# Weight conversion by VectorE and ScalarE alone, one and a half half chunks a step, in the order of use

## The chip, the core and the metric

The kernel runs on one core of a Trainium2 chip. TensorE (PE in the rows) multiplies matrices, VectorE (DVE), ScalarE (ACT) and GpSimd (POOL) work elementwise, and SyncE's queue (SP) issues the transfers from and to memory. Each engine takes its instructions in the order in which the program wrote them; waits between engines are semaphores. The metric is the device time of one execution in microseconds, median of several.

## What is computed

A block-causal attention (4 batches, 8 heads, 576 positions, head dimension 64, blocks of 64 positions), then two feed-forward layers on the 2304 x 512 result. Queries and keys come as float32, the weights as float64.

```python
def _attn_ref(q, k, v):
    scores = 1.0 / np.sqrt(D) * np.matmul(q, k.transpose(0, 1, 3, 2))
    scores = np.where(block_i >= block_j, scores, -1e9)   # blocks of 64
    attn = np.exp(scores - np.max(scores, axis=-1, keepdims=True))
    attn = attn / (np.sum(attn, axis=-1, keepdims=True) + 1e-09)
    return np.matmul(attn, v)

def _moe_ref(x, w_in, w_out):       # x 2304 x 512, w_in 512 x 2048, w_out 2048 x 512
    g = np.maximum(x @ w_in, 0.0) ** 2
    return g @ w_out

def _moe2_ref(x, w_in, w_out):
    h = x @ w_in
    return (h * np.cos(h)) @ w_out

def reference(**kwargs):
    x = _attn_ref(q, k, v)          # rearranged to 2304 x 512
    return _moe2_ref(_moe_ref(x, ...), ...)
```

## The kernel before

**Attention.** 16 pairs of heads are worked on one after another. Their steps (scores L358, maximum L370, exponential L375, scaling of P by GpSimd L411, transposes L432 with their two parts L437 and L440, weighted values L497, joins L508 to L517) are put in order by a planner, the class Plan: each step has an engine, a cost in microseconds and a rank, and each engine takes of the steps that can start the one of lowest rank. The first `EARLY = 8` half chunks of weights are converted among these steps (add_half), at a rank behind everything else.

**Feed-forward layers.** A layer's hidden units come in 16 chunks of 128, the tokens in blocks (512, 512, 256, 512 and 512 in the first layer, 512, 512, 512, 384 and 384 in the second). A step is one chunk of one block. TensorE does the hidden product of step s (L604, 12 products: four pieces of the model dimension, each as high x high, high x low and low x high) and then the output product of step s - 3 (L668, 12 products). ScalarE and VectorE do the activation between them: in the first layer relu and square (L626, L627), the high part of the result (L616, a cast on ScalarE, "gs high") and its low part (L619 on VectorE, "gs low"); the second layer has cosine work in five more steps. What step s leaves is taken up in steps s + 1 (ScalarE's) and s + 2 (gs low). At the end of a block the next one's values are cut into two parts (xs, L299 and L302), and the finished block is copied out of PSUM (L681, L687).

**Weights.** A float64 weight becomes two float32 parts. A chunk is converted in two halves, w_in's (h = 0, read by the hidden product) and w_out's (h = 1, read by the output product). For a half of 128 x 512 the steps are: load (SyncE), shift L201, mask L208, join L219, sign L231, power L237 (VectorE, integers; the words of a float64 lie side by side, so that these read or write every second word), rebias L214 and fraction L225 (ScalarE), and then on GpSimd the high part L246 (from bits) and the low part L252 (low word times high word). A call of convert() takes up to three halves one stage further: it finishes an old one, begins a new one, loads a third. The main loop calls it twice in each step of the first layer and once in a step of the second. The halves come chunk by chunk, w_in then w_out, first layer then second. Layer 2's weights take the tiles of layer 1's; a half of layer 2 may be begun once its chunk c is below freed[0], which is set after the last block's output product of the chunk:

```python
if begun[0].key >= (1, freed[0]):
    return
```

The loop at its core, before:

```python
if not (layer == 1 and c == LAG - 1):
    for _ in range(2 if layer == 0 else 1):
        convert()
```

In this document "the first layer" is layer 0 of the code and "the second" is layer 1.

## Time and profile before

| | us |
|---|---|
| median of 3 runs | 1051.83 |
| lowest and highest run | 1051.08, 1052.38 |
| span of the profiled execution | 1049.7 |
| TensorE busy | 997.2 (95%) |
| VectorE busy | 675.3 (64%) |
| ScalarE busy | 563.1 (54%) |
| GpSimd busy | 272.3 (26%) |

The profile is one execution; its span runs from its first to its last instruction. Busy shares are averages over stages that have different limits, so stages are read one by one: the attention lies at 0 to 209 us, the first layer at 209 to 635, the second from there to the end. Matmuls overlap, so a duration of 12 products is longer than the distance to the next group; distances between starts are what is added up.

### The profile page before, as it was taken

Reading aid. Unit: us, or ns where it says so; the run is one execution under the profiler, and the core shown is the slowest. Engines: PE = TensorE matmul, PEld = TensorE weight load, DVE = VectorE, ACT = ScalarE, POOL = GpSimd, SP = SyncE. Lnnn points to the kernel's source line nnn. Section 1 sums busy time; section 2 is a strip of 40 time slices with the busy share of each in tenths; the row PEclk is TensorE's granted clock in tenths of the full one; section 3 lists DMA queues with packets and bytes.
Section 4 is the critical chain, followed back from the end, with each engine's and each line's share of the span. In section 5 each row is a group of like instructions: output and inputs, shape, how many; then the busy total and the mean of one; then the engine's idle time right before and its main releaser. Section 6 shows DMA issues by size and latency. Waiting matters only on the chain.

```text
span 1049.7 us, 13810 instructions
## 1 busy us (share of the span) xinstructions
PE 997.2 (95%) x4895; PEld 825.7 (79%) x4895; DVE 675.3 (64%) x1244; ACT 563.1 (54%) x1166; POOL 272.3 (26%) x366
## 2 busy tenths in 40 slices
PE   9999999988799999999999887999999999999998
PEld 7766777776578889988888666778888888899997
DVE  7999998799971112121139999986555655565654
ACT  7999888865663334443345556544334433444433
POOL 6889988644420000000004443210000000000000
PEclk9999999999999999999999998999999999999999
DMA  6333222234420000000003443100100100000000
GB/s 232 123 125 134 94 94 93 94 119 136 143 84 1 1 1 1 1 1 1 1 1 120 142 140 110 51 1 1 41 1 1 41 1 1 9 32 1 31 1 30
DMA packets 18805, 58.56 MB, mean 56 GB/s; under 512 B 1968, under 2 KB 2096, under 8 KB 18736
## 3 DMA queue, kind: packets, MB, share of 16 engines
q1 hardware_dynamic: 18736, 57.68, 16.4%
q8 instruction: 38, 0.62, 0.3%
q14 instruction: 31, 0.25, 0.1%
HBM read 52.95 MB, written 4.72 MB: 55 GB/s over the span
## 4 chain that ended last, share of the span: by engine, by line
PE 61%; DVE 32%; ACT 3%; issue 1%; POOL 1%; DMA 0%; SPq 0%; DVEq 0%; ACTq 0%; POOLq 0%
PE acc L668 29%; PE h L604 28%; DVE raw L219 8%; DVE raw L237 4%; DVE bits L231 4%; DVE nmax L370 3%; DVE PTl L440 3%; DVE raw L201 2%; DVE bits L208 2%; DVE gs L619 2%; DVE sums L400 1%; PE ps L497 1%; PE ps L358 1%; DVE g L637 1%; PE ps L432 1%
## 5 line engine op out<-in xcount | busy, mean ns | idle before, releaser
L604 PE MATMUL h<-xs,w 128*128 128x512 f32 (+2 forms) x1920 | 423.6, 370 | 6.2 <-ACT xs L299 6.2
L604 PEld LDWEIGHTS h<-xs,w 128*128 128x128 f32 x1920 | 346.9, 189 | 63.2 <-issue 6.6
L668 PE MATMUL acc<-gs,w 128*128 128x512 f32 (+1 forms) x960 | 219.7, 376 | 23.4 <-DVE gs L619 23.4
L668 PEld LDWEIGHTS acc<-gs,w 128*128 128x128 f32 x960 | 169.5, 191 | 60.8 <-DVE gs L619 30.6
L668 PE MATMUL acc<-w,gs 128*128 128x512 f32 x864 | 211.1, 391 | 2.2 <-ACT xall L681 1.3
L619 DVE TENSOR_TENSOR gs<-g,gs 128x512 fp32r<-128x512 f32 (+2 forms) x160 | 101.0, 632 | 153.9 <-ACT gs L616 153.8
L668 PEld LDWEIGHTS acc<-w,gs 128*128 128x128 f32 x864 | 161.1, 188 | 36.9 <-DVE gs L619 2.1
L616 ACT CAST gs<-g 128x512 fp32r<-128x512 f32 (+2 forms) x160 | 92.2, 576 | 154.9 <-DVE g L651 95.6
L246 POOL TENSOR_SCALAR w<-bits 128x512 fp32r<-128x512 f32 x64 | 43.3, 677 | 362.0 <-DVE bits L231 357.1
L637 DVE SCALAR_TENSOR_TENSOR g<-turns,h 128x512 f32<-128x512 int32 (+1 forms) x80 | 50.5, 632 | 121.0 <-ACT turns L634 121.0
L219 DVE SCALAR_TENSOR_TENSOR raw<-raw 128x512 int32<-128x512 int32 x64 | 91.1, 1424 | 0.0
L358 PE MATMUL ps<-kB,qB 128*128 128x64 f32 (+7 forms) x256 | 83.0, 425 | 3.8 <-DVE PTl L440 1.0
L411 POOL TENSOR_SCALAR P<-P,rinv 128x64 f32<-128x64 f32 (+2 forms) x144 | 78.6, 563 | 25.5 <-DVE rinv L403 16.4
L214 ACT ACTIVATE bits<-bits,new_bias 128x512 int32<-128x512 int32 x64 | 46.3, 723 | 71.9 <-DVE bits L208 71.8
L626 ACT ACTIVATE g<-h 128x512 f32<-128x512 f32 (+1 forms) x80 | 43.9, 549 | 74.1 <-PE h L604 74.1
L634 ACT ACTIVATE turns<-h 128x512 int32<-128x512 f32 (+1 forms) x80 | 44.1, 552 | 69.1 <-PE h L604 69.0
L432 PEld LDWEIGHTS ps<-ident,P 128*128 128x128 f32 (+1 forms) x400 | 46.6, 139 | 38.7 <-DVE PTl L440 20.1
L252 POOL TENSOR_TENSOR w<-raw 128x512 fp32r<-128x512 f32 x64 | 69.4, 1085 | 23.9 <-issue 21.9
L648 ACT ACTIVATE g<-g,half_pi 128x512 f32<-128x512 f32 (+1 forms) x80 | 54.6, 682 | 37.2 <-DVE g L642 37.2
L375 ACT ACTIVATE P<-ps,nmax 128x64 f32<-128x64 f32 (+7 forms) x128 | 64.6, 506 | 17.5 <-DVE nmax L370 16.4
L432 PE MATMUL ps<-ident,P 128*128 128x128 f32 (+1 forms) x400 | 61.9, 277 | 7.8 <-DVE PTl L440 5.1
L440 DVE TENSOR_TENSOR PTl<-ps,PTh 128x512 fp32r<-128x512 f32 x96 | 64.1, 675 | 3.8 <-ACT PTh L437 3.6
(51 smaller groups left out, 1044.6 us busy)
## 6 DMA issues: line engine op xcount, KB each, us to landing
raw<-in_w_dram SPq DMA_DIRECT2D x64, 512.0 KB, 3.7
qB<-in_qd_dram SPq DMA_DIRECT2D x15, 576.0 KB, 5.1
v_raw<-in_vp_dram SPq DMA_DIRECT2D x16, 320.0 KB, 3.0
kB<-in_kT_dram SPq DMA_DIRECT2D x16, 288.0 KB, 3.2
out_dram<-o SPq DMA_DIRECT2D x8, 512.0 KB, 4.6
out_dram<-o SPq DMA_DIRECT2D x2, 256.0 KB, 2.9
qB<-in_qd_dram SPq DMA_DIRECT2D x1, 384.0 KB, 4.3
qB<-in_qd_dram SPq DMA_DIRECT2D x1, 192.0 KB, 2.9
```

What stands on the lines that cost most here:

```text
L219: nc.vector.scalar_tensor_tensor(out=self.low_word, in0=self.high_word, scalar=23, in1=self.low_word, op0=ALU.logical_shift_left, op1=ALU. ...
L252: nc.gpsimd.tensor_tensor(out=weights[(*self.key, self.h)][:, 1], in0=self.low_word.bitcast(F32), in1=self.high_word.bitcast(F32), op=ALU. ...
L358: nc.tensor.matmul(bank[:, 0:w] if one else wide[:, x, 0:w], lhsT=qB[r][:, i].rearrange("p e d -> p (e d)"), rhs=kB[r][:, x * w : (x + 1) ...
L375: nc.scalar.activation(out=mine if one else mine.rearrange("p (x w) -> p x w", x=2), in_=held(), func=AF.Exp, bias=nmax[i], scale=1.0, acc ...
L411: nc.gpsimd.tensor_scalar(out=mine, in0=mine, scalar1=inverse[:, i - i0 : i - i0 + 1], scalar2=1.0, op0=ALU.mult, op1=ALU.mult,)
L432: nc.tensor.transpose(bank[0:keys, n * 128 : (n + 1) * 128], P[r][:, o : o + keys], ident)
L440: nc.vector.tensor_tensor(out=PT[1][:, at] if keys == 128 else PT[0][keys:128, at], in0=bank[0:keys, 0:w], in1=PT[0][0:keys, at].bitcast(F32),
L604: nc.tensor.matmul(h, lhsT=w[:, a, kk * 128 : (kk + 1) * 128], rhs=xs[kk].parts[:, x], start=(m == 0), stop=(m == 3 * KD - 1),)
L616: nc.scalar.copy(out=gs[:, 0], in_=g)
L619: nc.vector.tensor_tensor(out=gs[:, 1], in0=g, in1=gs[:, 0].bitcast(F32), op=ALU.subtract)
L637: nc.vector.scalar_tensor_tensor(out=g, in0=turns, scalar=-part, in1=start, op0=ALU.mult, op1=ALU.add)
L668: nc.tensor.matmul(dst, lhsT=lhsT, rhs=rhs, start=(c == 0 and m == 0), stop=(c == KF - 1 and m == 2),)
```

## The change

- The high part of a half is a ScalarE copy and the low part a VectorE multiply; GpSimd has no part in the weights any more, neither in the attention's plan nor in the layers.
- The halves are sorted: w_out of chunk c comes beside w_in of chunk c + 3, ahead of it.
- The main loop calls convert() by a pace that adds up: 1.5 a step in the first and the last block of the first layer, 2 in its others, and in the second layer one every two steps.
- Room in the second layer is told by halves: w_in's tile of chunk c is free after the last block's hidden product, w_out's after its output product. The step in which the second layer made no call goes.
- Inside a call, the low part stands after the new half's mask and rebias.

```diff
     loads = [((layer, c), h) for layer in range(2) for c in range(KF) for h in range(2)]
+    loads.sort(key=lambda x: (x[0][0], x[0][1] + LAG * x[1], -x[1]))
     loads.reverse()
-    freed = [0]  # chunks of the second layer that have room
+    freed = [0, 0]
...
+        def room(self):
+            key = (*self.key, self.h)
+            if key not in weights:
+                pool = w_pools[0] if self.key[1] < NA else w_pools[1]
+                weights[key] = pool.tile(
+                    [128, 2, DM], F32R, tag=f"w{self.h}", name=f"w{self.h}"
+                )
+            return weights[key]
+
         def high(self):
...
-            nc.gpsimd.tensor_scalar(
-                out=w[:, 0], in0=self.bits.bitcast(F32), scalar1=1.0, scalar2=0.0,
-                op0=ALU.mult, op1=ALU.add,
-            )
+            nc.scalar.copy(out=self.room()[:, 0], in_=self.bits.bitcast(F32))
 
         def low(self):
-            nc.gpsimd.tensor_tensor(
-                out=weights[(*self.key, self.h)][:, 1], in0=self.low_word.bitcast(F32),
+            nc.vector.tensor_tensor(
+                out=self.room()[:, 1], in0=self.low_word.bitcast(F32),
                 in1=self.high_word.bitcast(F32), op=ALU.mult,
             )
...
         if begun:
-            if begun[0].key >= (1, freed[0]):
+            (layer, c), h = begun[0].key, begun[0].h
+            if layer == 1 and c >= freed[h]:
                 return
...
         if old:
             old.power()
             old.high()
-            old.low()
         if new:
             new.mask()
             new.rebias()
+        if old:
+            old.low()
+        if new:
             new.join()
             later.append(new.fraction)
...
-                plan.add("G", 0.59, rank, x.high, [bits])
-                plan.add("G", 1.45, rank, x.low, [raw, high])
+                plan.add("A", 0.56, rank, x.high, [bits])
+                plan.add("V", 0.6, rank, x.low, [raw, high])
...
+        PACE = {0: 1.5, last: 1.5}
+        owed = 0.0
...
-            if not (layer == 1 and c == LAG - 1):
-                for _ in range(2 if layer == 0 else 1):
-                    convert()
+            if step < len(steps) and i == last:
+                freed[0] = c + 1
+            owed += PACE.get(i, 0.5 if layer == 1 else 2)
+            while owed >= 1:
+                owed -= 1
+                convert()
...
                 if i == last:
-                    freed[0] = c + 1
+                    freed[1] = c + 1
```

**VectorE, first block of the first layer.** Here raw and bits are the words of a half on its way, gs the activation; before, one step from gs low to gs low holds two halves:

```order
L619 TENSOR_TENSOR gs_2305<-g_2304,gs_2305 128x512
L231 SCALAR_TENSOR_TENSOR bits_2373<-raw_2364,bits_2373 128x512
L201 TENSOR_SCALAR raw_2377<-raw_2377 128x512
L237 TENSOR_SCALAR raw_2364<-bits_2373 128x512
L208 TENSOR_SCALAR bits_2404<-raw_2377 128x512
L219 SCALAR_TENSOR_TENSOR raw_2377<-raw_2377 128x512
L231 SCALAR_TENSOR_TENSOR bits_2404<-raw_2377,bits_2404 128x512
L201 TENSOR_SCALAR raw_2408<-raw_2408 128x512
L237 TENSOR_SCALAR raw_2377<-bits_2404 128x512
L208 TENSOR_SCALAR bits_2417<-raw_2408 128x512
L219 SCALAR_TENSOR_TENSOR raw_2408<-raw_2408 128x512
L619 TENSOR_TENSOR gs_2348<-g_2347,gs_2348 128x512
```

and with the change a step with one call (the step before it has two such groups of six):

```order
L627 TENSOR_TENSOR gs_2335<-g_2334,gs_2335 128x512
L233 SCALAR_TENSOR_TENSOR bits_2390<-raw_2382,bits_2390 128x512
L203 TENSOR_SCALAR raw_2395<-raw_2395 128x512
L239 TENSOR_SCALAR raw_2382<-bits_2390 128x512
L210 TENSOR_SCALAR bits_2433<-raw_2395 128x512
L257 TENSOR_TENSOR w0_2431<-raw_2382 128x512
L221 SCALAR_TENSOR_TENSOR raw_2395<-raw_2395 128x512
L627 TENSOR_TENSOR gs_2366<-g_2365,gs_2366 128x512
```

The low part (L257, the w row) has joined VectorE's queue, one in each half; line numbers are those of either file (L203, L210, L221, L233 and L239 are the old L201, L208, L219, L231 and L237).

**ScalarE, the same block.** A step with two halves before, from relu to relu:

```order
L626 ACTIVATE g_2503<-h2_2263 128x512
L627 ACTIVATE g_2503<-g_2503 128x512
L225 ACTIVATE raw_2520<-raw_2520 128x512
L616 CAST gs_2504<-g_2503 128x512
L214 ACTIVATE bits_2572<-bits_2572,new_bias_59 128x512
L225 ACTIVATE raw_2533<-raw_2533 128x512
L214 ACTIVATE bits_2585<-bits_2585,new_bias_59 128x512
```

and a step with two calls in the changed kernel:

```order
L634 ACTIVATE g_2520<-h3_2264 128x512
L635 ACTIVATE g_2520<-g_2520 128x512
L227 ACTIVATE raw_2494<-raw_2494 128x512
L624 CAST gs_2521<-g_2520 128x512
L254 CAST w0_2573<-bits_2532 128x512
L216 ACTIVATE bits_2575<-bits_2575,new_bias_59 128x512
L227 ACTIVATE raw_2537<-raw_2537 128x512
L254 CAST w1_2586<-bits_2575 128x512
L216 ACTIVATE bits_2588<-bits_2588,new_bias_59 128x512
```

The cast of each half's high part (L254) stands between the fraction of its half and the rebias of the next; w0 and w1 alternate, w0 for a later chunk than w1.

**VectorE in the attention.** The stretch at row 266 of its queue, around the join of a pair's values, before:

```order
L237 TENSOR_SCALAR raw<-bits 128x512
L201 TENSOR_SCALAR raw<-raw 128x512
L511 TENSOR_TENSOR xall<-ps_85,half_117 64x320
L208 TENSOR_SCALAR bits<-raw 128x512
L219 SCALAR_TENSOR_TENSOR raw<-raw 128x512
L370 TENSOR_REDUCE nmax_105<-ps_83 128x1
L201 TENSOR_SCALAR raw<-raw 128x512
L440 TENSOR_TENSOR PTl<-ps_86,PTh 128x512
```

and with the change:

```order
L239 TENSOR_SCALAR raw<-bits 128x512
L203 TENSOR_SCALAR raw<-raw 128x512
L519 TENSOR_TENSOR xall<-ps_86,half_117 64x320
L257 TENSOR_TENSOR w_1341<-raw 128x512
L378 TENSOR_REDUCE nmax_105<-ps_87 128x1
L210 TENSOR_SCALAR bits<-raw 128x512
L221 SCALAR_TENSOR_TENSOR raw<-raw 128x512
L378 TENSOR_REDUCE nmax_106<-ps_85 128x1
```

The multiply for a half (L257) stands among the maxima and joins, and the halves on their way are at another stage than before. In the whole attention the queue holds eight such rows; the last stands after row 380 of some 440, where the last conversion row was 325 of 430.

## Rows read from the trace of the kernel before

Timeline rows are: start (us), duration (us), engine, line, operation, out<-in, partitions x elements and type, count; in brackets the idle time before it and what ended it.

**Rows 1.** The page, section 2: VectorE's busy tenths in 40 slices of 26.24 us.
```profile
DVE  7999998799971112121139999986555655565654
```

**Rows 2.** Windows: length; busy us of PE, PEld, DVE, ACT, POOL; clock; DMA; GB/s.
```profile
26.25:157.50 131.25, 120.41 (x718) 92.98 (x716) 126.46 (x282) 118.07 (x331) 114.57 (x156) 1.00 0.34 114
157.50:209.00 51.50, 48.17 (x305) 38.48 (x303) 43.26 (x103) 44.48 (x125) 40.85 (x59) 1.00 0.28 95
209.04:304.97 95.93, 80.10 (x327) 62.34 (x326) 91.89 (x136) 57.23 (x95) 44.23 (x49) 0.96 0.40 132
635.25:640.23 4.98, 4.98 (x12) 3.71 (x13) 4.98 (x9) 1.96 (x4) 1.41 (x2) 0.56 0.04 16
```

**Rows 3.** Timeline, TensorE, the first layer's first block.
```profile
222.73 2.88 PE L604 MATMUL h<-xs,w 128*128 128x512 f32 x12
...
234.37 2.79 PE L668 MATMUL acc<-gs,w 128*128 128x512 f32 x11 [1.81 <-DVE gs L619]
...
304.97 2.88 PE L604 MATMUL h<-xs,w 128*128 128x512 f32 x12
...
310.41 2.88 PE L604 MATMUL h<-xs,w 128*128 128x512 f32 x12
```

**Rows 4.** Timeline, TensorE, from the first layer's last block into the second layer.
```profile
585.11 2.88 PE L604 MATMUL h<-xs,w 128*128 128x512 f32 x12
...
635.25 5.14 PE L604 MATMUL h<-xs,w 128*128 128x512 f32 x12 [6.22 <-ACT xs L299]
...
689.71 2.88 PE L604 MATMUL h<-xs,w 128*128 128x512 f32 x12
...
696.02 2.88 PE L604 MATMUL h<-xs,w 128*128 128x512 f32 x12
...
701.47 2.88 PE L604 MATMUL h<-xs,w 128*128 128x512 f32 x12
```

**Rows 5.** Timeline, all engines: one half chunk's conversion in the first block.
```profile
264.44 0.68 DVE L231 SCALAR_TENSOR_TENSOR bits<-raw,bits 128x512 int32<-128x512 int32 x1
...
264.85 0.60 ACT L616 CAST gs<-g 128x512 fp32r<-128x512 f32 x1
265.04 0.42 DVE L201 TENSOR_SCALAR raw<-raw 128x512 int32<-128x512 int32 x1
265.21 0.73 POOL L246 TENSOR_SCALAR w<-bits 128x512 fp32r<-128x512 f32 x1 [1.84 <-DVE bits L231]
265.38 0.84 DVE L237 TENSOR_SCALAR raw<-bits 128x512 int32<-128x512 int32 x1
266.14 0.41 DVE L208 TENSOR_SCALAR bits<-raw 128x512 int32<-128x512 int32 x1
266.36 1.09 POOL L252 TENSOR_TENSOR w<-raw 128x512 fp32r<-128x512 f32 x1 [0.42 <-issue]
266.47 1.53 DVE L219 SCALAR_TENSOR_TENSOR raw<-raw 128x512 int32<-128x512 int32 x1
...
267.92 0.68 DVE L231 SCALAR_TENSOR_TENSOR bits<-raw,bits 128x512 int32<-128x512 int32 x1
...
268.52 0.42 DVE L201 TENSOR_SCALAR raw<-raw 128x512 int32<-128x512 int32 x1
```

**Rows 6.** Timeline, the same stretch earlier: L219 with no GpSimd operation beside it.
```profile
212.95 0.68 DVE L219 SCALAR_TENSOR_TENSOR raw<-raw 128x512 int32<-128x512 int32 x1
...
213.96 1.04 POOL L252 TENSOR_TENSOR w<-raw 128x512 fp32r<-128x512 f32 x1 [1.54 <-ACT raw L225]
```

**Rows 7.** Line L231 in the attention: count, duration ns least/median/most, first and last start.
```profile
L231 DVE SCALAR_TENSOR_TENSOR bits<-raw,bits x8: 670/778/1201, 37.7 to 153.6; 128x512 int32<-128x512 int32 x8
```

**Rows 8.** Timeline, VectorE, attention: a pair's widest maximum, one in each pair.
```profile
34.80 0.74 DVE L370 TENSOR_REDUCE nmax<-wide 128x1 f32<-128x576 f32 x1
...
166.00 0.74 DVE L370 TENSOR_REDUCE nmax<-wide 128x1 f32<-128x576 f32 x1
...
189.76 0.75 DVE L370 TENSOR_REDUCE nmax<-wide 128x1 f32<-128x576 f32 x1
```

More of the change, by code (lines that the diff above doesn't have):

```diff
@@ L183, in tile_block_causal_attention__then__two_ffn @@
     weights = {}
+    LAG = 3
     loads = [((layer, c), h) for layer in range(2) for c in range(KF) for h in range(2)]
+    loads.sort(key=lambda x: (x[0][0], x[0][1] + LAG * x[1], -x[1]))
     loads.reverse()
     loaded, begun = [], []
-    freed = [0]
+    freed = [0, 0]
     class Half:
@@ L240, in power @@
             )
-        def high(self):
-            pool = w_pools[0] if self.key[1] < NA else w_pools[1]
-            w = pool.tile([128, 2, DM], F32R, tag=f"w{self.h}", name=f"w{self.h}")
-            weights[(*self.key, self.h)] = w
-            nc.gpsimd.tensor_scalar(
-                out=w[:, 0], in0=self.bits.bitcast(F32), scalar1=1.0, scalar2=0.0,
-                op0=ALU.mult, op1=ALU.add,
-            )
+        def room(self):
[6 more added lines that the diff above has]
+            return weights[key]
+        def high(self):
+            nc.scalar.copy(out=self.room()[:, 0], in_=self.bits.bitcast(F32))
         def low(self):
-            nc.gpsimd.tensor_tensor(
-                out=weights[(*self.key, self.h)][:, 1], in0=self.low_word.bitcast(F32),
+            nc.vector.tensor_tensor(
+                out=self.room()[:, 1], in0=self.low_word.bitcast(F32),
                 in1=self.high_word.bitcast(F32), op=ALU.mult,
@@ L700, in layers @@
         steps = [(i, c) for i in range(len(blocks)) for c in range(KF)]
-        LAG = 3
+        PACE = {0: 1.5, last: 1.5}
+        owed = 0.0
         gss = {}
```

## Prediction

> **What bounds the kernel now.** I began with the page's busy digits in 40 slices [rows 1]. VectorE stands at 9 in three stretches: in the attention (slices 2 to 6), in slices 9 to 11 and in 22 to 26. Then the table of windows [rows 2] put the other engines beside it. Over the first block of the first layer, 209.04 to 304.97, VectorE is busy 91.89 of 95.93 us and TensorE only 80.10; so VectorE sets the pace there, and in the attention's middle it does so at 126.46 of 131.25 us.
>
> The TensorE timeline says what a feed-forward step costs when nothing holds it: from 304.97 to 310.41, 5.44 us (24 products of 512 columns) [rows 3]. In the first block the steps are further apart, and the wait named in front of the output products is gs low, VectorE's last operation on a step's activations: 1.81 us in this row, the same in most steps. From step 4 (222.73) to step 15 (304.97) eleven steps take 82.24 us; at 5.44 they take 59.84. **22.4 us** are lost there. The same happens around the seam of the layers [rows 4]: from step 10 of the first layer's last block (585.11) to step 11 of the second layer's first block (701.47) lie 17 steps in 116.36 us, against 92.48: **23.9 us**. A piece of this is the wait of 6.22 us for the next block's xs at 635.25; TensorE had stood still before it, the granted clock of the next stretch is 0.56 [rows 2], near the level of 1.2 GHz, and twelve products took 5.14 us instead of 2.88. Between these stretches TensorE runs at its pace, and nothing is to be had.
>
> Why VectorE is late stands in a VectorE, GpSimd and ScalarE timeline of one half chunk [rows 5]. VectorE starts L201 at 265.04 and the next half's L201 at 268.52: 3.48 us for a half of five operations. L237 takes 0.84 us where L201 and L208, the same form, take 0.42 and 0.41: GpSimd's L246 runs beside it. L219 takes 1.53 us beside GpSimd's L252. In [rows 6] L219 starts at 212.95 and is over before L252 starts at 213.96: 0.68 us. So GpSimd's two operations per half cost VectorE about 0.85 and 0.42 us, which is more than they would take on VectorE.
>
> **The change part by part.** *Conversion on VectorE and ScalarE.* L246 becomes a cast on ScalarE, priced by the cast of gs, same shape, 0.60 us [rows 5]. L252 becomes a two-input multiply on VectorE, whose nearest row is L231 (two inputs, 128x512), 0.68 us and 0.60 to the next start [rows 5]. Its inputs are every second word; L219 reads and writes like that and takes the same 0.68 [rows 6]. Bounds: 0.41 (L208) and 1.53 (L219 beside GpSimd, [rows 5]); I take 0.60, since no GpSimd is left in the layers. From start to start a half is then 0.60 (L231) + 0.34 (L201) + 0.34 (L237) + 0.34 (L208) + 0.60 (multiply) + 0.60 (L219) = 2.82 us instead of 3.48.
>
> *1.5 half chunks a step.* Before, two: 2 x 3.48 + 0.60 (gs low, also of two inputs) = 7.56 us a step, which is the pace seen. With the change 1.5 x 2.82 + 0.60 = **4.83 us**, under 5.44. A step with two calls takes VectorE 6.24, one with one call 3.42; a gs low is queued a whole step before its product, which covers the 0.8. ScalarE was busy 57.23 us over this stretch with 24 halves; 24 casts of 0.60 make 71.6 of about 79 (four hidden products and one output, then twelve steps of 5.44): high, but under TensorE's time. What stands behind a waiting cast there is the next chunk's relu, whose own product ends later.
>
> *The order of halves.* Slowed to 1.5, the weights must come as the products ask for them. w_in of chunk c is now the (2c-1)th half, w_out of chunk c-3 the one before. Eight are ready at the start, two calls fill the pipe, so after step 12 there are 17, after step 13 19, after step 14 20; steps 13, 14 and 15 ask for 17, 19 and 21, so step 15 forces one more call, ahead of its product. A half cut in step s is done some 3 us into TensorE's step s, 2.4 us before step s+1. So block 0 loses nothing: **-22.4 us**. The loads keep their number on SP's queue, and the fourth raw buffer is free about two calls ahead, as before.
>
> *Room by halves, in the last block.* The first halves of layer 2 wait on hidden products of the same step (chunks 0, 1, 2); behind that wait stand ScalarE's relu, which needs the same product, and a gs low that is due two steps later, so nothing is lost. Three calls return empty; then 1.5 a step, 21 halves at the block's end, and the other 11 in layer 2 at one in two steps. There a step with one half took 6.31 us, from 689.71 to 696.02 [rows 4]; less 3.48 and plus 1.41 it is 4.24, under 5.44. The wait for xs goes too: that cast stands in ScalarE's queue behind the step's conversions, which were late by the pace of 7.56 us a step; at TensorE's pace ScalarE reaches it when step 15's hidden product ends. What is late next is w_out of chunks 14 and 15, which are cut in the very step that uses them, behind VectorE's 4.24 us of work: I put 1.3 us on it, with bounds of nothing and of a whole step, 5. **-23.9 + 1.3**.
>
> *Attention.* Eight halves are cut there, and eight multiplies and eight casts move from GpSimd. With conversion a pair of heads takes (166.00 - 34.80) / 10 = 13.12 us, without it (189.76 - 166.00) / 2 = 11.88 [rows 8]. VectorE is 96% busy in the first case and 84% from 157.50 on [rows 2], so the eight multiplies lie on the path: 8 x 0.60 = 4.8 us. Upper bound: GpSimd still scales P there, and L231, of the same kind, took 0.67 to 1.20 us [rows 7]: 9.6 us. Lower bound: the new order spreads the halves into the pairs after 157.50, where 8.2 us of VectorE lie idle; and 16 GpSimd operations fewer (1.09 and 0.73 us, [rows 5]) relieve what is left, so a gain of 2 us is the other end. The casts, 8 x 0.60 = 4.8 us, go to ScalarE, busy 90% there [rows 2], 8.4 us less than VectorE, so it stays second. I take **+4.5 us**, near the plain 4.8.
>
> *The Trainium skill on this.* The Trainium skill's page SBUF — State Buffer, section "SBUF: two separate sides", says that VectorE and GpSimd share a pair of ports under an exclusive lock, held for the whole instruction, so that whoever comes second waits. By that rule L219 would have ended 0.68 us after L252, at 268.13; the row [rows 5] ends at 268.00, so the trace nearly agrees. The rule speaks against the change in the attention, where GpSimd works on: each multiply could wait out a whole operation, and by 1.09 + 0.68 us for each of eight the attention would pay 14.2 us, the whole sum 1021.
>
> Sum: 1051.83 - 22.4 - 23.9 + 1.3 + 4.5 = **1011.3 us**. The profiled execution has a span of 1049.7, 2.1 under the median of the runs; its stretches are taken off the median as they are.
>
> **The rivals.** *The attention pays double.* Each multiply is held by a GpSimd operation and takes the 1.20 us of [rows 7], and the casts lengthen the same chain: 9.6 + 4.8 us instead of 4.5. For it: VectorE at 96%. Against: L231's median is 0.78, and a pair with conversion is only 1.24 us longer than one without. It gives 1016 to 1021.
>
> *1.5 is too much.* ScalarE at 71.6 of 79 us and VectorE at 4.83 of 5.44 hand each other six results a half; if each of some 27 steps lost half a microsecond, 13.5 us come back: 1025. Against it: before, VectorE ran without a gap at 91.89 of 95.93 us through the same exchange.
>
> *The slow operations are slow by themselves.* If L219 stays at 1.53 and L237 at 0.84 without GpSimd, a half is 3.48 + 0.60 and a step 6.72: block 0 loses 11 x 1.28 = 14.1 and the last block 16 x 1.28 = 20.5 of what is hoped for: 1046. The change then does not do what it says. [rows 6] speaks against it.
>
> *Slower: the room wait closes into a ring.* In the last block the cast and the multiply for chunk c wait for hidden product c on in-order engines. If every step were held like that, its round would be half a step for the hidden product (2.72), five ScalarE operations of about the cast's 0.60 (cast of w, L214, relu, square, cast of gs; 3.0), 0.68 (gs low, as L231) and 2.72 (output), 9.12 us: 3.7 lost in each of 16 steps, 60 us, so 1071. It is slower than before from 2.5 us a step on. Against it: after chunk 2 the room that a half takes was freed one to three steps earlier.
>
> **How the numbers follow.** The forecast 0.62; attention dearer 0.17; 1.5 too much 0.12; slow by themselves 0.05; ring 0.04. The forecast's own spread is 1003.5 (attention -2 and nothing late at the end) to 1020 (attention 9.6, 5 late at the end); I round the lower end to 1004, since both would have to come together. With the first rival whole and most of the second the range is 1004 to 1023. A measurement here tells 0.2%, 2 us. All cases but the last are faster by more: 0.95 faster, 0.01 same, 0.04 slower.
>
> **What the changed kernel's profile would show.** L219's successor at about 0.68 and L237's at 0.41 in the layers; hidden products 5.44 us apart from step 4 on in block 0, and across the seam, with the granted clock at 1.00; no GpSimd after the attention; first hidden product at about 213.5 instead of 209.04. It is wrong if the products still wait for gs low each step, if they wait for w (L246's or L252's successor), or if the attention ends after 219.

## The result and the profile after

| | before | after |
|---|---|---|
| median us | 1052.11 (4 runs beside it) | **1007.55** (4 runs, 1006.25 to 1009.78) |
| ratio, 95% interval | 1 | 0.9578 [0.9564, 0.9592] |
| span of the profiled execution | 1049.7 | 1005.0 |
| TensorE busy, share of the span | 95% | 98% |
| first hidden product at | 209.04 | 207.22 |

The forecast was 1011.3, with a range of 1004 to 1023. The changed file is a little longer, so that lines move: L201 is now L203, L208 L210, L219 L221, L231 L233, L237 L239, L246 L254, L252 L257, L604 L612, L619 L627, L668 L676.

The page of the changed kernel, section 2 (busy tenths in 40 slices of 25.1 us) and section 4 (shares of the chain that ended last):

```profile
DVE  7999999979972121211168979788656645656554
POOL 6878887720000000000000000000000000000000
PEclk9999999999999999999999999999999999999999
...
PE 79%; DVE 14%; ACT 4%; issue 1%; POOL 0%; DMA 0%; SPq 0%; DVEq 0%; ACTq 0%; POOLq 0%
```

VectorE still shows 9 in the attention, as in [rows 1]; at the first block two slices are left of three, at the seam two of five. GpSimd is silent from slice 10 on. The chain runs over TensorE for 79% of the span and over VectorE for 14%, most of the latter in the attention. The windows of the changed kernel give the same stretch by stretch (length, then busy us of PE, PEld, DVE, ACT and POOL, the granted clock, the DMA's share, GB/s):

```profile
26.25:157.50 131.25, 123.53 (x740) 96.00 (x739) 125.51 (x291) 123.68 (x347) 109.64 (x147) 1.00 0.35 117
157.50:207.20 49.70, 45.01 (x286) 36.32 (x285) 45.04 (x103) 42.47 (x118) 38.01 (x51) 1.00 0.27 92
207.22:302.51 95.29, 95.29 (x423) 78.92 (x422) 82.44 (x169) 78.98 (x136) 0.87 (x1) 1.00 0.40 133
```

In the third stretch, which is about as long as the one of [rows 2], TensorE is now busy for all of 95.29 us and VectorE for 82.44; there it was 80.10 and 91.89 of 95.93. It is no longer the first block alone, since that now ends at 286.19; up to there VectorE is busy for 71.66 of 78.97 us. In the attention VectorE has hardly moved, 125.51 of 131.25 us against 126.46.

TensorE's timeline of the changed kernel, at step 4 of the first block and across the seam of the layers, the places of [rows 3] and [rows 4] (start, duration, engine, line; a bracket would be a wait):

```profile
220.91 2.88 PE L612 MATMUL h<-xs,w 128*128 128x512 f32 x12
223.63 2.88 PE L676 MATMUL acc<-gs,w 128*128 128x512 f32 x12
226.35 2.88 PE L612 MATMUL h<-xs,w 128*128 128x512 f32 x12
...
626.17 2.88 PE L612 MATMUL h<-xs,w 128*128 128x512 f32 x12
628.89 2.88 PE L676 MATMUL acc<-w,gs 128*128 128x512 f32 x12
631.61 2.88 PE L612 MATMUL h<-xs,w 128*128 128x512 f32 x12
```

Hidden products start 5.44 us apart, here and in every step from 220.91 to 686.01 whose two products have 512 tokens (once 5.47, at a block's start); the wait for gs and the wait for xs are gone. Then one step stalls. TensorE with what VectorE and ScalarE do ahead of it, in the second layer's first block:

```profile
686.01 2.88 PE L612 MATMUL h<-xs,w 128*128 128x512 f32 x12
...
689.20 0.68 DVE L627 TENSOR_TENSOR gs<-g,gs 128x512 fp32r<-128x512 f32 x1
...
689.80 0.68 DVE L233 SCALAR_TENSOR_TENSOR bits<-raw,bits 128x512 int32<-128x512 int32 x1
...
690.52 0.62 ACT L254 CAST w<-bits 128x512 fp32r<-128x512 f32 x1 [0.42 <-DVE bits L233]
...
691.19 0.50 PE L676 MATMUL acc<-w,gs 128*128 128x512 f32 x1 [2.30 <-ACT w L254]
...
692.15 2.79 PE L676 MATMUL acc<-w,gs 128*128 128x512 f32 x11 [0.45 <-DVE w L257]
...
694.78 2.88 PE L612 MATMUL h<-xs,w 128*128 128x512 f32 x12
```

From hidden product to hidden product this step takes 8.77 us instead of 5.44, so 3.33 are lost. The output product asks for a half that is cut in this very step: its L233 starts at 689.80, behind nine operations of the activation that stand ahead of it in VectorE's queue from 683.86 on (the last is the L627 at 689.20).

**Where the time went.** Three numbers of a trace account for the span of nearly every kernel in this study: when the first hidden product starts, what the first block loses against 5.44 us a step, and what the stretch from the first layer's last block to the end of the second layer's first block loses (the seam of the layers lies in it). What is left of the span is 794.3 to 794.5 us in all but one kernel.

| kernel | median us | ratio, 95% interval | first hidden | lost, block 0 | lost, seam and layer 2 | span |
|---|---|---|---|---|---|---|
| before | 1052.1 | | 209.04 | 22.4 | 23.9 | 1049.7 |
| after | 1007.55 | [0.9564, 0.9592] | 207.22 | 0 | 3.4 | 1005.0 |
| a1_new_order_gpsimd | 1006.97 | [0.9556, 0.9582] | 205.32 | 0 | 5.0 | 1005.2 |
| a2_old_order_new_engines | 1009.98 | [0.9585, 0.9616] | 209.28 | 0 | 3.3 | 1007.0 |
| b1_pace_order_room_gpsimd | 1027.36 | [0.9750, 0.9779] | 209.57 | 12.1 | 8.5 | 1024.6 |
| b2_engines_alone | 1021.48 | [0.9693, 0.9722] | 209.59 | 7.9 | 7.4 | 1019.3 |
| b3_pace2 | 1018.65 | [0.9667, 0.9699] | 207.14 | 7.7 | 6.2 | 1015.5 |
| b4_chunk_order | 1015.37 | [0.9637, 0.9665] | 207.15 | 3.8 | 7.3 | 1012.7 |
| b5_old_room | 1018.15 | [0.9661, 0.9687] | 207.09 | 0 | 15.1 | 1016.5 |
| c1_tail | 1003.19 | [0.9519, 0.9545] | 207.04 | 0 | 0 | 1001.4 |
| c2_gpsimd_beside | 1051.59 | [0.9982, 1.0001] | 206.92 | 25.0 | 23.8 | 1050.0 |
| e1_gpsimd_attention_tail | **1001.68** | [0.9507, 0.9533] | 205.68 | 0 | 0 | 1000.0 |
| e2_early6 | 1001.89 | [0.9511, 0.9537] | 201.89 | 3.9 | 0 | 1000.1 |
| e3_early7 | 1001.89 | [0.9504, 0.9530] | 204.88 | 1.0 | 0 | 1000.3 |

(In a1 the rest is 794.9. The half microsecond more lies behind the last hidden product: from there to the end of the span it is 15.67 us, against 15.14 in the changed kernel. c2's 25.0 has in it 1.1 us of two steps of the second block.) From before to after: 22.4 + 23.9 - 3.4 + 1.8 = 44.7 us, the difference of the spans.

### The profile page after: what moved, and what is told of

The parts are those of the page before. It is cut to its first block, busy times and chain, and to the rows that moved or that the text cites. A ratio compares the mean times of both kernels' runs of the same rounds, so it can differ in the third digit from the quotient of the medians.

```text
span 1005.0 us, 13762 instructions
## 1 busy us (share of the span) xinstructions
PE 982.7 (98%) x4895; PEld 823.0 (82%) x4895; DVE 642.6 (64%) x1308; ACT 595.4 (59%) x1230; POOL 165.1 (16%) x238
## 4 chain that ended last, share of the span: by engine, by line
PE 79%; DVE 14%; ACT 4%; issue 1%; POOL 0%; DMA 0%; SPq 0%; DVEq 0%; ACTq 0%; POOLq 0%
PE h L612 38%; PE acc L676 38%; DVE nmax L378 4%; DVE PTl L448 4%; ACT P L383 1%; PE ps L366 1%; ACT PTh L445 1%; PE ps L505 1%; DVE sums L408 1%; ACT half L516 1%; PE ps L440 1%; DVE g L645 1%; DVE xall L519 1%; DVE raw L203 1%; DVE xs L310 1%
## 5 line engine op out<-in xcount | busy, mean ns | idle before, releaser
L612 PE MATMUL h<-xs,w 128*128 128x512 f32 (+2 forms) x1920 | 420.7, 368 | 0.0
L612 PEld LDWEIGHTS h<-xs,w 128*128 128x128 f32 x1920 | 344.6, 188 | 55.2
L676 PE MATMUL acc<-w,gs 128*128 128x512 f32 x864 | 210.1, 391 | 2.8 <-ACT w L254 2.3
L676 PE MATMUL acc<-gs,w 128*128 128x512 f32 (+1 forms) x960 | 210.2, 368 | 0.0
L676 PEld LDWEIGHTS acc<-gs,w 128*128 128x128 f32 x960 | 168.3, 189 | 30.0
L627 DVE TENSOR_TENSOR gs<-g,gs 128x512 fp32r<-128x512 f32 (+2 forms) x160 | 101.3, 634 | 142.4 <-ACT gs L624 142.2
L676 PEld LDWEIGHTS acc<-w,gs 128*128 128x128 f32 x864 | 161.6, 188 | 35.7 <-ACT w L254 2.7
L419 POOL TENSOR_SCALAR P<-P,rinv 128x64 f32<-128x64 f32 (+2 forms) x144 | 81.7, 584 | 34.1 <-DVE rinv L411 19.8
L505 PE MATMUL ps<-PTh,vhl 128*128 128x320 f32 (+3 forms) x224 | 60.5, 304 | 3.6 <-POOL vhl L480 1.4
L445 ACT CAST PTh<-ps 128x512 fp32r<-128x512 f32 (+1 forms) x112 | 58.8, 543 | 1.1 <-PE ps L440 0.5
L378 DVE TENSOR_REDUCE nmax<-ps 128x1 f32<-128x64 f32 (+7 forms) x128 | 55.4, 445 | 6.0 <-PE ps L366 5.5
```

What stands on the lines that cost most here:

```text
L378: nc.vector.tensor_reduce(out=nmax[i], in_=held(), axis=AX.X if one else AX.XY, op=ALU.max, negate=True)
L419: nc.gpsimd.tensor_scalar(out=mine, in0=mine, scalar1=inverse[:, i - i0 : i - i0 + 1], scalar2=1.0, op0=ALU.mult, op1=ALU.mult,)
L445: nc.scalar.copy(out=PT[0][0:keys, at], in_=plan.held[s][0][0:keys, 0:w])
L505: nc.tensor.matmul(bank[:, (a - i0) * D : w], lhsT=vhl[:, j, e].rearrange("p x d -> p (x d)"), rhs=pt[x][:, s0 : s0 + i1 - a, e, :], start ...
L612: nc.tensor.matmul(h, lhsT=w[:, a, kk * 128 : (kk + 1) * 128], rhs=xs[kk].parts[:, x], start=(m == 0), stop=(m == 3 * KD - 1),)
L627: nc.vector.tensor_tensor(out=gs[:, 1], in0=g, in1=gs[:, 0].bitcast(F32), op=ALU.subtract)
```

## Experiment 1: is it GpSimd's presence that made a half slow?

c2 takes the changed kernel and lets GpSimd do its two former operations again, in the layers, into a tile that nobody reads. VectorE and ScalarE still make the weights.

```diff
+    idle = const.tile([128, DM], F32R, name="idle")
...
             old.high()
+            nc.gpsimd.tensor_scalar(out=idle, in0=old.bits.bitcast(F32), ...)
+            nc.gpsimd.tensor_tensor(out=idle, in0=old.low_word.bitcast(F32), ...)
```

> The changed kernel with GpSimd's two former operations issued again in every call of the layers, on the same inputs, into a tile that nobody reads. Theory (GpSimd running beside VectorE is what made a half dear): the join takes 1.5 us and the power 0.84 again, a half 4.1 us, a step of 1.5 halves 6.7 us; 14 us are lost in the first block and 20 in the last, about 1042. Rival (the operations were dear for where they stood, not for GpSimd): they stay at 0.68 and 0.42, 1008.

Measured: 1051.59 us, all of the gain gone. One half of c2 in the first block, VectorE and GpSimd, and TensorE's wait behind it (here L240 is the power, L222 the join, L258 the multiply, L636 gs low):

```profile
240.23 0.65 POOL L286 TENSOR_SCALAR idle<-bits 128x512 fp32r<-128x512 f32 x1 [1.31 <-DVE bits L234]
240.32 0.84 DVE L240 TENSOR_SCALAR raw<-bits 128x512 int32<-128x512 int32 x1
...
241.40 1.59 POOL L290 TENSOR_TENSOR idle<-raw 128x512 fp32r<-128x512 f32 x1 [0.52 <-DVE raw L240]
241.41 0.68 DVE L258 TENSOR_TENSOR w<-raw 128x512 fp32r<-128x512 f32 x1
...
242.01 1.53 DVE L222 SCALAR_TENSOR_TENSOR raw<-raw 128x512 int32<-128x512 int32 x1
...
244.20 1.20 PE L685 MATMUL acc<-gs,w 128*128 128x512 f32 x4 [2.27 <-DVE gs L636]
```

The join takes 1.53 us again and the power 0.84, the same two numbers as in [rows 5], while the multiply of the same half keeps its 0.68. In the changed kernel one half in the second layer, VectorE alone:

```profile
671.07 0.69 DVE L233 SCALAR_TENSOR_TENSOR bits<-raw,bits 128x512 int32<-128x512 int32 x1
671.67 0.42 DVE L203 TENSOR_SCALAR raw<-raw 128x512 int32<-128x512 int32 x1
672.01 0.42 DVE L239 TENSOR_SCALAR raw<-bits 128x512 int32<-128x512 int32 x1
672.34 0.42 DVE L210 TENSOR_SCALAR bits<-raw 128x512 int32<-128x512 int32 x1
672.68 0.69 DVE L257 TENSOR_TENSOR w<-raw 128x512 fp32r<-128x512 f32 x1
673.28 0.68 DVE L221 SCALAR_TENSOR_TENSOR raw<-raw 128x512 int32<-128x512 int32 x1
```

So the slowness is the neighbour's, not the operation's: the rival "slow by themselves" fell. The price of a half is as expected: from L234 at 239.39 to the next at 244.06 lie 4.67 us with one gs low of 0.60 in them, so a half of c2 costs VectorE 3.48 + 0.60 us, six operations of which two are slowed, and a step of 1.5 halves 6.7. The loss is larger than expected, 25.0 and 23.8 us instead of 14 and 20, and the time 1051.59 instead of 1042. I had multiplied the 1.28 us by which a step exceeds 5.44 by the number of steps; Experiment 2 shows at b1 why that is the wrong sum. Summed as it is done there, 12 steps of 6.72 - 4.83 us make 22.7, and the 22nd join of the block stands at 304.51, 24.1 us behind the changed kernel's 280.37.

## Experiment 2: one part of the change at a time

Four kernels take one part out, or bring one alone. b1 has the new pace, order and room, but GpSimd finishes every half as before:

```diff
-            old.high()
+            old.high_g()
+            old.low_g()
...
-        if old:
-            old.low()
```

> The change's pace of 1.5, its order of halves and its room, with the two last steps of a half on GpSimd as before, in the attention and in the layers (the attention in its old order). Theory (the pace takes off most of the loss by itself, the engines take off the rest): a half is 3.48 us of VectorE as before, a step 1.5 x 3.48 + 0.60 = 5.82 us, 0.38 over TensorE's 5.44, so block 0 gives back some 4 us, the last block some 6, the attention ends at 209 again (+1.8): about 1020. Rival (the engines are what counts, as the run with idle GpSimd work suggests, which lost all 44 us): 1035 to 1050. Rival (pace, order and room do everything): 1009.

b2 is the kernel before with the new engines in the layers alone:

```diff
-            nc.gpsimd.tensor_scalar(out=w[:, 0], in0=self.bits.bitcast(F32), ...)
+            nc.scalar.copy(out=self.room()[:, 0], in_=self.bits.bitcast(F32))
...
-            nc.gpsimd.tensor_tensor(out=weights[(*self.key, self.h)][:, 1], ...)
+            nc.vector.tensor_tensor(out=self.room()[:, 1], ...)
```

> The kernel before with one part of the change: in the layers the high part of a half is ScalarE's cast and the low part VectorE's multiply. Pace 2, order by chunks, room by chunks and the attention stay as before. Theory: a half is 2.82 us, a step 2 x 2.82 + 0.60 = 6.24 us, 0.80 over TensorE's 5.44. Block 0 loses 11 x 0.80 = 9 of the 22.4 us, the last block with the seam 16 x 0.8 = 13 of the 23.9: about 1052 - 46.3 + 22 = 1028. Rival (the slow operations of the half weren't GpSimd's doing): 1052 or more, since VectorE then has one operation more in a half. Rival (engines alone suffice, the pace is nothing): 1007 to 1012.

b3 is the changed kernel at the old pace:

```diff
-        PACE = {0: 1.5, last: 1.5}
+        PACE = {}
```

> The changed kernel with two calls a step in the whole first layer instead of 1.5 in its first and last block. Theory: a step with two halves is 2 x 2.82 + 0.60 = 6.24 us of VectorE, 0.80 over 5.44. In block 0, 24 halves are cut in 12 steps instead of 16, then 0.8 x 12 = 9.6 us are lost; in the last block room limits it, some 13 steps of 0.8, 10: about 1007.5 + 15 to 20 = 1022 to 1027, with the half chunks of the second layer earlier and its stall of 3.3 us gone. Rival (the order and the engines suffice): 1004 to 1008.

b4 leaves the halves in the old order, b5 frees w_in's room as late as w_out's:

```diff
-    loads.sort(key=lambda x: (x[0][0], x[0][1] + LAG * x[1], -x[1]))
```

> The changed kernel with the halves in the old order, chunk by chunk, w_in then w_out, at the pace of 1.5. Theory: w_in of chunk c is then the (2c + 1)th half instead of the (2c - 1)th from chunk 3 on, wanted in step c; of the eight ready at the start and 1.5 a step the wanted half is behind from about step 10 on, and calls are forced just ahead of a product, each half the length of a late half (4 to 5 us): three to four of them in block 0, some in layer 2's first block: 1015 to 1025. Rival (the order doesn't matter): 1007 to 1009.

```diff
-            if step < len(steps) and i == last:
-                freed[0] = c + 1
...
-                    freed[1] = c + 1
+                    freed[0] = freed[1] = c + 1
```

> The changed kernel with room in the second layer told as before: w_in's tile counts as free only after the last block's output product of its chunk, three steps later than the hidden product. Theory (the room by halves is needed): three steps of 1.5 calls return empty, so some four to five halves fewer are ready at the seam, and the second layer, which is given one half in two steps, falls behind the products earlier, at its step 10 or so; from there each step takes two halves, some 3 us more than 5.44 each, four to six of them: 1018 to 1024. Rival (the room by halves is not needed, the forced calls hide): 1006 to 1009.

Measured: engines alone 1021.48, everything but the engines 1027.36, both together 1007.55. Either takes off more than half of the 44 us; they overlap, since both lower VectorE's work in a step. Neither is enough alone. Nor is any part without effect: at two halves a step the kernel stands at 1018.65, in the old order at 1015.37, with the old room at 1018.15.

What each leaves behind is to be seen on TensorE. In b2 and b3 VectorE sets the step again, at 6.24 us (2 x 2.82 + 0.60, as expected), and at the seam the next block's xs is late once more. TensorE of b2, first block and seam:

```profile
244.58 2.79 PE L685 MATMUL acc<-gs,w 128*128 128x512 f32 x11 [0.49 <-DVE gs L636]
...
250.81 2.83 PE L685 MATMUL acc<-gs,w 128*128 128x512 f32 x11 [0.50 <-DVE gs L636]
...
608.21 5.79 PE L621 MATMUL h<-xs,w 128*128 128x512 f32 x12 [4.21 <-ACT xs L316]
```

The two output products lie 6.23 us apart. The last block itself lost nothing in b2 or b3 (its steps stand 5.44 apart up to the seam): VectorE runs late there without TensorE's waiting, and the bill comes with xs, 4.21 us in the row, with twelve products in 5.79 us behind it. That fits what the prediction said of xs at the seam, that it is late by VectorE's and ScalarE's backlog. Since I had counted 0.80 us for each step of the last block, both kernels came out cheaper than expected (1028 for b2, 1022 to 1027 for b3).

In b4 the steps of the first block are 6.22 apart from step 11 on (the row below is of step 12): each of them forces a second half ahead of its product, and TensorE waits for w, not for gs. In b5 the loss of 15.1 us is all behind the seam, where four steps take 7.65 to 11.40 us. Three of them have a wait for w of 2.42 to 2.69 us, like the changed kernel's stall; in the fourth (7.65) it is mostly the clock, ten products in 4.13 us at a granted 0.61 that take 2.56 elsewhere. TensorE of b4:

```profile
266.14 2.56 PE L611 MATMUL h<-xs,w 128*128 128x512 f32 x10 [0.22 <-DVE w L256]
```

b1 is where a step of my reckoning failed. I expected 0.38 us lost in each step of the first block (1.5 x 3.48 + 0.60 = 5.82), some 4 in all. VectorE did keep that pace: its joins at 221.27 and 291.05 are twelve steps apart, 5.82 each. But the block lost 12.1 us. GpSimd and TensorE of b1:

```profile
270.61 0.72 POOL L254 TENSOR_SCALAR w<-bits 128x512 fp32r<-128x512 f32 x1 [1.84 <-DVE bits L233]
...
271.39 0.73 PE L623 MATMUL h<-xs,w 128*128 128x512 f32 x2 [1.35 <-POOL w L254]
...
271.75 1.09 POOL L260 TENSOR_TENSOR w<-raw 128x512 fp32r<-128x512 f32 x1 [0.42 <-issue]
...
272.89 3.86 PE L623 MATMUL h<-xs,w 128*128 128x512 f32 x10 [0.77 <-POOL w L260]
```

TensorE waits for w, the half just cut. (The ten products of the last row take 3.86 us, 2.57 in other steps; the granted clock there is 0.63.) The products ask for two halves a step and VectorE makes one and a half; the eight in stock pay for the rest, and they are used up at the block's end. And VectorE has no idle time to take a loss from: in the changed kernel, too, it runs without a gap from 212.81 to 270.79, with one of 1.14 us behind that. So a loss on any of the halves comes out at the end nearly in full: the changed kernel's VectorE needs 4.83 us a step, b1's 5.82, and 12 steps of 0.99 are 11.9 us. The 22nd join of the block is at 294.53 in b1 and at 280.37 in the changed kernel, 14.2 us apart; the next block's first hidden product is at 300.68 and 286.19, 14.5 apart, and 2.4 of it are the later start of the layers. What decides is the sum of VectorE's work up to the last half that is wanted, not its surplus over 5.44 in a single step.

## Experiment 3: the attention, by its order or by its engines?

The attention was to cost 4.5 us more and ended 1.8 us earlier. The planner was given new engines and costs for the eight halves, and so it also wrote another order. a1 keeps the new order but lets GpSimd finish the halves; a2 keeps the old order (the planner is told the old engines and costs) but lets ScalarE and VectorE finish them. Both have the changed kernel's layers.

```diff
 a1
-                plan.add("A", 0.56, rank, x.high, [bits])
-                plan.add("V", 0.6, rank, x.low, [raw, high])
+                plan.add("A", 0.56, rank, x.high_g, [bits])
+                plan.add("V", 0.6, rank, x.low_g, [raw, high])
 a2
-                plan.add("A", 0.56, rank, x.high, [bits])
-                plan.add("V", 0.6, rank, x.low, [raw, high])
+                plan.add("G", 0.59, rank, x.high, [bits])
+                plan.add("G", 1.45, rank, x.low, [raw, high])
```

> The changed kernel with the attention's eight halves finished on GpSimd again, in the changed kernel's order of steps on every other engine. Theory (work taken off GpSimd frees VectorE, so the engines are what shortened the attention): the first hidden product starts later than 207.2 us, at 209 to 211, and the whole is 1009 to 1011. Rival (the planner's other order is what helped): it starts at 207 or before, the whole is 1007.5 or less. The layers are as in the changed kernel in both.

> The changed kernel with the attention's steps planned as before (order of the kernel before), the eight halves finished on ScalarE and VectorE. Theory (engines): the first hidden product starts at about 207, the whole is 1007 to 1008. Rival (order): it starts at 209 or later, the whole is 1009.5 or more.

Measured, the first hidden products, in this order a2, the changed kernel, a1 (three traces):

```profile
209.28 11.13 PE L612 MATMUL h<-xs,w 128*128 128x512 f32 x48
```

```profile
207.22 11.13 PE L612 MATMUL h<-xs,w 128*128 128x512 f32 x48
```

```profile
205.32 11.13 PE L624 MATMUL h<-xs,w 128*128 128x512 f32 x48
```

With before's 209.04 that is a table of two by two, and other runs repeat three of its cells. The old order with GpSimd gave 209.57 and 209.59 too (b1, b2), the new order with the new engines 206.92 to 207.22 (six kernels), the new order with GpSimd 205.68 too (e1). So the same attention varies by up to 0.55 us, and by that measure:

- the new order gains 2.1 to 2.4 us with ScalarE and VectorE, and 3.4 to 4.3 with GpSimd;
- the new engines cost 1.2 to 1.9 us in the new order, and nothing that can be told from the spread in the old one.

So the earlier end is the order's. The engines gained nothing; they cost at most 1.9 us, less than the 4.5 that I put on them.

*Where the order's gain is.* The last of the eight halves (its power, the last operation that all four kernels have) starts at 154.9 us before and at 154.7 in a2, but at 175.9 in the changed kernel and at 174.5 in a1. The planner, which now counts 0.6 us of VectorE for each, spreads them over some 21 us more, into the stretch in which [rows 2] left 8.2 us of VectorE idle. TensorE is further on by then: up to 157.50 it has been busy for 123.53 us in the changed kernel, 120.41 in [rows 2] and 121.20 in a2. No run moves the halves and leaves the rest of the order alone, so that this place of the gain is argued and not shown.

*Why eight multiplies cost so little.* In a2 VectorE is as busy from 26.25 to 157.50 as before, 126.25 us against 126.46, though seven multiplies are new there. The groups of VectorE's operations in that stretch (count, busy us, mean ns, idle before), first two of a2, then one of before:

```profile
L257 DVE TENSOR_TENSOR w<-raw 128x512 fp32r<-128x512 f32 x7 | 5.3, 757 | 0.0
...
L408 DVE TENSOR_SCALAR sums<-sums 128x4 f32<-128x4 f32 x10 | 4.3, 427 | 0.1
```

```profile
L400 DVE TENSOR_SCALAR sums<-sums 128x4 f32<-128x4 f32 x10 | 7.2, 720 | 0.1
...
L403 DVE RECIPROCAL rinv<-sums 128x4 f32<-128x4 f32 x10 | 1.8, 178 | 1.0
```

The multiplies cost 5.3 us. An operation on four columns took 720 ns on average and takes 427; over ten pairs that gives back 2.9 us, its sisters on two and three columns 1.3, the conversion's own operations the rest. The reciprocal of the same four columns takes 178 ns, so that most of the 720 should be a wait and no work. The trace of before shows the wait, here at its longest:

```profile
80.37 1.54 POOL L472 TENSOR_TENSOR vhl<-v_raw,vhl 128x640 fp32r<-128x640 f32 x1
...
80.48 1.45 DVE L400 TENSOR_SCALAR sums<-sums 128x4 f32<-128x4 f32 x1
```

GpSimd's operation ends at 81.91 and VectorE's at 81.93. Of the 29 operations on sums that start in this stretch, nine take 0.15 to 0.17 us; of the 20 longer ones 18 end 0.02 to 0.04 us behind a GpSimd operation that ran beside them. In 14 of these 18 that was an operation of the attention itself, as in this row, and not the weights' work. So it matters when GpSimd's operations fall more than how many there are: in a1, where GpSimd is busy for 115.91 us of the stretch (114.57 before), the operation on four columns takes 280 ns. What the sums gave back in a2 is therefore at least in part a shift in time, which the prediction had not reckoned.

The Trainium skill, page SBUF — State Buffer, section "SBUF: two separate sides", has a lock between VectorE and GpSimd: whoever starts first keeps the shared pair for a whole instruction. The prediction priced this as a rival that makes each multiply wait, 14.2 us. The multiplies' mean of 757 ns against 0.68 us alone shows that they hardly waited. The sums' ends agree with the rule; the waits that vanished from them were not in that price.

## Experiment 4: the stall in the second layer

c1 cuts a little more in the second layer's first block, so that the last half is ready before its step:

```diff
-        PACE = {0: 1.5, last: 1.5}
+        PACE = {0: 1.5, last: 1.5, last + 1: 0.75}
```

> The changed kernel with 0.75 instead of 0.5 calls a step in the second layer's first block, so that the last two w_out halves are cut a step or more before their products. Theory (the wait of 2.3 us for w in step 17 and the 0.45 and 0.6 us beside it is a half cut too late): step 17 takes 5.44 us instead of 8.77, the whole is 3.3 us shorter, 1004.3. Rival (VectorE is full there anyhow, 2.83 + 0.75 x 2.82 = 4.95 of 5.44 us, and other steps lose it): 1006 to 1008.

Measured: 1003.19 us (1002.87 to 1003.38). TensorE of c1, the place of the stall:

```profile
685.84 2.88 PE L612 MATMUL h<-xs,w 128*128 128x512 f32 x12
688.56 2.88 PE L676 MATMUL acc<-w,gs 128*128 128x512 f32 x12
691.28 2.88 PE L612 MATMUL h<-xs,w 128*128 128x512 f32 x12
694.00 2.88 PE L676 MATMUL acc<-w,gs 128*128 128x512 f32 x12
696.72 2.88 PE L612 MATMUL h<-xs,w 128*128 128x512 f32 x12
```

The step is 5.44 us again. The medians differ by 4.4 us, more than the 3.4 of the trace. A part of the rest is TensorE's clock: two of the changed kernel's four executions ran at a mean granted clock of 1.000 (1006.73 and 1006.25 us), one at 0.998 (1008.37) and one at 0.996 (1009.78). In a1's profile such a fall is to be seen in this very place. Its TensorE, then the window with the granted clock (the number before the last two):

```profile
689.30 0.50 PE L688 MATMUL acc<-w,gs 128*128 128x512 f32 x1 [2.30 <-ACT w L266]
690.25 4.37 PE L688 MATMUL acc<-w,gs 128*128 128x512 f32 x11 [0.46 <-DVE w L269]
```

```profile
690.00:695.00 5.00, 4.75 (x14) 3.75 (x15) 4.82 (x10) 3.40 (x6) 0.00 (x0) 0.66 0.00 0
```

TensorE stood still twice, for 2.30 and 0.46 us, and then did eleven products in 4.37 us that take 2.79 at full clock; the granted 0.66 is a mean between the levels of 1.2 and 2.4 GHz. The same two waits stand in the changed kernel's profile, at a granted clock of 1.00. So the same stall cost 4.9 us in one execution and 3.3 in the other, which, with the half microsecond behind its last product, is why a1 began its layers 1.9 us earlier and ended no earlier.

## Experiment 5: what is left in the attention

If that reading holds, GpSimd in the attention and no stall should add up. e1 is a1 with c1's pace:

> The changed kernel with GpSimd finishing the eight halves of the attention (as in a1_new_order_gpsimd) and with 0.75 half chunks a step in the second layer's first block (as in c1_tail). a1_new_order_gpsimd reached its first hidden product 1.9 us earlier than the changed kernel but lost that in its wait at the end of the second layer's first block, where the granted clock fell to 0.66 in 5 us. Theory (the earlier start is real and the clock at that wait ate it): without the wait it keeps the 1.9 us, so 1003.2 - 1.9 = 1001.3. Rival (the earlier start is taken back by something else later): 1003.2.

Measured: 1001.68 us (1001.34 to 1002.08), against c1's 1003.19. They add up: the first hidden product is 1.4 us earlier than in c1 (205.68 and 207.04), nothing is lost behind it, and the spans differ by the same 1.4. It is the lowest median of the study. Then fewer halves were cut in the attention and more in the first block, on top of e1:

```diff
 e2
-    EARLY = 8
+    EARLY = 6
-        PACE = {0: 1.5, last: 1.5, last + 1: 0.75}
+        PACE = {0: 1.7, last: 1.5, last + 1: 0.75}
 e3
-    EARLY = 8
+    EARLY = 7
-        PACE = {0: 1.5, last: 1.5, last + 1: 0.75}
+        PACE = {0: 1.6, last: 1.5, last + 1: 0.75}
```

> As e1_gpsimd_attention_tail, with six half chunks instead of eight cut in the attention and 1.7 a step instead of 1.5 in the first block. Theory (a half costs the attention about 1.2 to 1.5 us, and the first block has VectorE to spare: 1.7 x 2.82 + 0.60 = 5.39 us of 5.44): 2.4 to 3 us better than e1, 998.5. Rival (5.39 of 5.44 leaves nothing for a late start, and w comes late to the products): 1001 to 1006.

> As e1_gpsimd_attention_tail, with seven half chunks cut in the attention and 1.6 a step in the first block. e2_early6 began the hidden products 3.8 us earlier and lost 3.8 in the block, where two halves more are 5.6 us of VectorE; so e1 has 5.6 - 3.8 = 1.8 us of VectorE to spare in that block. Theory (that is the account): one half less begins 1.9 us earlier and loses 2.8 - 1.8 = 1.0 in the block, so 0.9 less than e1_gpsimd_attention_tail, 1000.8. Rival (what is saved in the attention is lost in the block, half for half): 1001.7. Rival (all of the earlier start is kept, since the loss begins only with the eighth half): 999.8.

Measured: 1001.89 for both, no difference from e1. In e2 the layers begin 3.8 us earlier and lose 3.9 us in the first block, where TensorE waits for weights:

```profile
254.44 3.02 PE L624 MATMUL h<-xs,w 128*128 128x512 f32 x12 [0.61 <-ACT w L266]
...
260.44 3.05 PE L624 MATMUL h<-xs,w 128*128 128x512 f32 x12 [0.26 <-ACT w L266]
```

Two more halves in the block are 5.6 us of VectorE, of which 1.8 found room: that is the block's reserve. For e3 that reserve foretold a loss of 2.8 - 1.8 = 1.0, and 1.0 was measured. What I had wrong was its gain: the seventh half taken out of the attention shortened it by 0.8 us, not by half of what two did. So in these three kernels what the attention gains the first block loses. By that, less VectorE work up to some 285 us would help, wherever it stands; no run here tried it.

## Why the prediction came out, point by point

- **The layers, -22.4 and -23.9.** Right, to a tenth. The half at 2.82 us, the step at 4.83 and the 5.44 between hidden products are in the trace: VectorE's joins at 218.44 and 247.38 are nine halves and six steps apart, 4.82 us a step. The successors of L219 and L237 take 0.68 and 0.42. b2 shows the same prices at two halves a step. But 4.83 under 5.44 is not what makes the first block's loss nothing, as b1 shows; what does is that the last half wanted is cut in time, which the prediction reckoned apart, by counting halves. The reserve is small: 1.8 us over the whole block by e2, not 0.6 in each step.
- **The late halves at the end, +1.3 with bounds of 0 and 5.** The mechanism and the place were right (w_out of chunk 14, cut in the step that uses it, by the wait for w); the size was 3.3. I took VectorE's 4.24 us of work in such a step and let most of it run beside the hidden product. But the half stands at the end of the queue, behind nine operations of activation from 683.86 to 689.80, one of which waits for ScalarE; what counts is when that queue comes to the half, and TensorE was done at 688.89.
- **The attention, +4.5 with bounds of -2 and 9.6.** The mis-sized term: -1.8, at the edge of its bounds. I took the plain price of eight multiplies, because VectorE was 96% busy. Of the two things named at the lower bound, the new order is worth 2.1 us (a2 to after), and in the old order VectorE's other operations give back what the multiplies cost, but no more (209.28 in a2, 209.04 to 209.59 without the new engines). Busy time in [rows 2] held waits on GpSimd; it was not all work, so adding work to it did not simply add time.
- **Order, pace, room.** Each was said to be needed or free of cost; b3, b4 and b5 show that leaving one out costs 8 to 11 us. That w_in comes as the (2c-1)th half and that the waiting conversions hold up nobody is borne out by 5.44 us in each step.
- **The rivals.** "Slow by themselves" fell by c2; "1.5 is too much" by VectorE's 82.44 of 95.29 us; the ring of room waits by the last block's undisturbed 5.44; "the attention pays double" by a2.

The sum foretold 40.5 us and the spans differ by 44.7: one term was 6.3 us too dear, one 2.0 too cheap, and they partly cancel. That the time came out 3.8 us from the forecast, and no further, is owed in part to that.

## What to carry to other kernels

Where two engines slow each other, take the price of an operation from a row without the neighbour, and move the work even to the busier one: six operations cost VectorE less alone than five beside GpSimd. Where the neighbour works on anyway, this need not hold: in the attention GpSimd was the better place for the same two operations, by 1.2 to 1.9 us in the new order. When a stock is drawn down while work is paced, add up the producer's work to the last piece that is wanted instead of comparing one step with another, and cut each piece a step ahead of its use, since one that is cut in the step itself waits for all that is queued before it.

## What the runs showed of the hardware

- A small operation of VectorE can wait out a whole one of GpSimd: on the 128 x 2 to 128 x 4 sums of the attention it takes 0.15 to 0.17 us at best and up to 1.45, and before, 18 of the 20 long ones end 0.02 to 0.04 us behind a GpSimd operation. How busy GpSimd is does not settle it: the mean on four columns is 720 ns before, 427 in a2 and 280 in a1, with GpSimd busy for 114.57, 104.73 and 115.91 of 131.25 us.
- The slowed integer operations end later than that behind GpSimd's: the join 0.55 us, the power 0.28, both in [rows 5] and in c2, less than the 0.68 and 0.42 that they take alone.
- Slowing goes both ways: GpSimd's two-input operation takes 1.09 us in [rows 5] and 1.59 in c2 (its spans are rough), where VectorE's multiply starts 0.01 us behind it and keeps its 0.68.
- The same wait of 2.8 us in two parts was followed by full clock in one execution (after) and by 0.66 over 5 us in another (a1). b5 has both in one execution: behind a wait of 2.47 us ten products took 2.60 us at a granted 1.00, behind one of 2.42 us 4.13 at 0.61. The stall's price is not fixed.
